# Issuing the first gate and value weights behind the third pair's cast instead of the fourth's

## The chip, the cores and the metric

The kernel runs on one core of a Trainium2 chip. The metric is the device time of one execution in microseconds; the time of a kernel is the median of its runs. Five engines work side by side, each through its own queue in order: TensorE (PE, with its weight loads PEld), VectorE (DVE), ScalarE (ACT), GpSimd (POOL) and SyncE (SP, which here only issues DMAs). POOL issues DMAs too: those that cast float32 to float16 on the way.

## The reference

Two attentions over the same q, k and v are added, and the sum goes through a gated feed-forward layer. Shapes: 8 batches, 8 heads, 576 positions, head size 64; the layer takes 4608 tokens of 512 through 1536 hidden columns.

```python
q_d = q.reshape(B, H, Sd, 4, D).mean(axis=3)      # k_d, v_d alike
out_up = np.repeat(sm_attn(q_d, k_d, v_d), 4, axis=2)
mask = np.abs(pos[:, None] - pos[None, :]) < 4
attn = softmax(np.where(mask, scale * q @ k.T, -1e9))
attn_out = out_up + attn @ v
x = attn_out.transpose(0, 2, 1, 3).reshape(B * S, H * D)
out = (np.maximum(x @ w_gate, 0.0) * (x @ w_val)) @ w_out
```

## The kernel before

The attention goes over 32 pairs of heads, four to a batch, numbered 0 to 31. For each pair: q and k are loaded (SP), cast to float16 and put in order (L1330 or L1329, tile `c`, for the first four pairs staged in `gT` and `wo_sb`), transposed (L1456 on PE for the first eight pairs, by DMA after that), copied out (`qkT`), summed over four positions (`qkd`), and multiplied to scores, local (L1518) and downsampled (L1537). The local scores become `s_sb` (minus the maximum), `e` (exponential) and are divided by their sum at L1610; the downsampled ones become `nmb` (L1590, the bias of the exponential), `wd` and are divided at L1626. `e` is turned by DVE (L1616, tile `at`), `wd` by PE (L1635) into `wT`. The value windows are 96 KB loads of small rows (L1675, tile `vw`, four a pair), cast at L1330 or L1329. The last product of a pair is L1726 with L1734; its result is added into `xT` (L1754).

The feed-forward layer takes tokens in stretches. A step is one of 128 hidden columns: four matmuls with gate weights and four with value weights (L1793, tiles `wg_sb` and `wv_sb`), the rectifier on ACT (L1807, tile `r`), the product on DVE (L1814, tile `gT`). Then 128 tokens at a time are multiplied with the output weights (L1859, `wo_sb`) and copied out (L1868). The stretch of batch 0 needs pairs 0 to 3, the next one pairs 4 to 7, and so on. The first two steps begin with the three pairs that are there (the columns of pairs 0 to 2) and add pair 3's columns later. The casts of pairs 4 to 7 wait for the divisions and for `wT` of pair 3.

The weights come by POOL in pieces: four of the gate (384 columns each), four of the value, four of the output. `W_AT` gives each pair of gate and value pieces the planned time before which it may not be issued.

The order on every engine is made when the kernel is built: `list_schedule` takes each operation with a duration, its dependencies, a rank (`prio`) and perhaps an earliest time (`after`). It steps through planned time and takes, on the engine that can start soonest, the lowest rank among what is ready. `RANKS` is a table of shifts by name added to the ranks (pair 3's cast has -489). Where an operation can run on several engines, the planner chooses the one that would end it first. The same order is then written out on each engine's queue.

Names used below: pair p's cast, its divisions (L1610 for `e`, L1626 for `wd`), its windows' cast (`vw`), its last product. "The second stretch" begins with the first gate step after batch 0's tokens.

Of the kernel before, what the change touches and what calls it, by code (L numbers as in the profile page):

```python
# [48 lines left out]

DMA_START = {SP: 0.8, POOL: 2.2}  # L50
RECEIPT = 1.2
W_AT = (20.0, 30.0, 34.0, 38.0)
WO_T0, WO_DT = 52.0, 6.0

PACE = (-10, -6, -5, 0)
# [1166 lines left out]
def kernel(  # L1222
# [90 lines left out]
    def add(*a, **kw):  # L1313
        o = Op(*a, **kw)
        ops.append(o)
        return o
# [62 lines left out]
    def wpiece(dst, src, c0, n):  # L1379
        return lambda o: nc.gpsimd.dma_start(  # L1380
            out=dst[:, :, c0 : c0 + n],
            in_=_dap(src, c0, [[DFF, 128], [128 * DFF, 4], [1, n]]))
# [6 lines left out]
    for g in range(4):  # L1389
        for nm, dst, src in (("g", wg_sb, moe_w_gate), ("v", wv_sb, moe_w_val)):  # L1390
            w_ld[nm, g] = add(POOL, 0.85, wpiece(dst, src, 384 * g, 384), prio=-40 + g,
                              xfer=2.55, after=W_AT[g], name=f"w{nm}{g}", port=(POOL,))

# [565 lines left out]
```

## Time and profile before

| what | us |
|---|---|
| median of three runs | 366.89 |
| lowest, highest run | 366.61, 369.45 |
| the profiled execution's own time | 368.73 |
| its span, first to last instruction | 367.0 |
| PE busy in the span | 352.3 |
| DVE, ACT, POOL busy | 254.4, 206.1, 199.6 |

The profile is one execution. Its span is 1.7 us shorter than its own time, and its own time is 1.8 us above the median; a change is worked out as a difference to 368.73 and then taken off the median. In the rows of the timeline the columns are start, duration, engine, line, operation, output<-input, shapes, count, and in brackets the idle time before it with what ended it. TensorE's granted clock was 1.00 throughout.

### The profile page before, as it was taken

The numbers are of one execution on the slowest core, as the hardware profiler recorded it, in microseconds if no ns is written. First come the engines' busy times: TensorE is split into PE (matmuls) and PEld (weight loads), VectorE is DVE, ScalarE is ACT, GpSimd is POOL, SyncE is SP. The second block draws the span as 40 slices with busy tenths as digits, with TensorE's granted clock in tenths as the row PEclk, the third lists the DMA queues.
The fourth block names the chain that finished last, engine by engine and source line by source line (L and its number), as shares of the span: only waits on it lengthen the run. The fifth ranks groups of instructions, "written<-read, shape, count | busy, mean of one in ns | idle before, by whom it ended". The sixth has DMA issues, their size and how long they took to land.

```text
span 367.0 us, 10494 instructions
## 1 busy us (share of the span) xinstructions
PE 352.3 (96%) x4238; PEld 181.9 (50%) x4238; DVE 254.4 (69%) x482; ACT 206.1 (56%) x481; POOL 199.6 (54%) x235
## 2 busy tenths in 40 slices
PE   7787999889999999999999999999989999999996
PEld 3444645445554554545444445544544454445554
DVE  4675999946889698878885986788968863322210
ACT  2576686436875657665466575768558533323222
POOL 7689566731567979675877469476885310000000
DMA  7999999669999999999999999999995121011012
GB/s 185 216 266 228 195 171 325 102 131 193 287 188 206 194 319 171 251 210 274 192 171 223 239 282 166 224 270 181 215 222 112 24 79 59 0 60 52 5 66 108
DMA packets 122067, 64.80 MB, mean 177 GB/s; under 512 B 100386, under 2 KB 106402, under 8 KB 122018
## 3 DMA queue, kind: packets, MB, share of 16 engines
q1 hardware_dynamic: 116194, 59.41, 74.8%
q0 software_dynamic: 5824, 4.72, 8.3%
q8 instruction: 33, 0.54, 0.7%
q14 instruction: 16, 0.13, 0.1%
HBM read 47.59 MB, written 9.44 MB: 155 GB/s over the span
## 4 chain that ended last, share of the span: by engine, by line
PE 78%; DMA 11%; DVE 4%; POOL 2%; issue 1%; ACT 1%; SPq 1%; POOLq 0%; ACTq 0%
PE bank L1793 49%; PE bank L1859 19%; DMA wg_sb<-in_moe_w_gate_dram 3%; DMA vw<-in_v_dram 3%; PE bank L1518 3%; PE bank L1726 2%; DMA tq<-c 2%; PE bank L1734 2%; DMA wT<-wd 2%; DMA sums_sb<-sums 1%; PE bank L1537 1%; DVE e L1610 1%; DVE vw L1352 1%; PE bank L1838 1%; DVE wd L1626 1%
## 5 line engine op out<-in xcount | busy, mean ns | idle before, releaser
L1814 DVE TENSOR_TENSOR gT<-r,bank 128x512 f16<-128x512 f16 (+1 forms) x112 | 74.5, 667 | 65.2 <-PE bank L1793 61.6
L1793 PE MATMUL bank<-xT,wg_sb 128*128 128x512 f16 (+2 forms) x528 | 112.1, 341 | 1.3 <-DMA wg_sb<-in_moe_w_gate_dram 1.3
L1793 PE MATMUL bank<-xT,wv_sb 128*128 128x512 f16 (+2 forms) x528 | 112.1, 341 | 0.8 <-ACT r L1807 0.8
L1807 ACT ACTIVATE r<-bank 128x512 f16<-128x512 f32 (+1 forms) x112 | 65.2, 583 | 64.1 <-PE bank L1793 57.8
L1859 PE MATMUL bank<-wo_sb,gT 128*128 128x512 f16 x420 | 96.7, 379 | 0.0
L1793 PEld LDWEIGHTS <-wg_sb 128*128 128x128 f16 x528 | 43.8, 98 | 48.0 <-DMA wg_sb<-in_moe_w_gate_dram 1.8
L1793 PEld LDWEIGHTS <-wv_sb 128*128 128x128 f16 x528 | 44.2, 98 | 46.2 <-issue 2.0
L1859 PEld LDWEIGHTS <-gT 128*128 128x128 f16 x420 | 39.9, 98 | 45.3 <-issue 0.4
L1868 ACT COPY y_sb<-bank 128x512 f32<-128x512 f32 x35 | 20.5, 586 | 47.9 <-PE bank L1859 45.6
L1330 POOL CAST vw<-vw 128x1536 f16<-128x1536 f32 x26 | 38.1, 1466 | 4.5 <-issue 1.4
L1506 DVE TENSOR_REDUCE qkd<-qkT 128x288 f16<-128x1152 f16 x28 | 37.5, 1339 | 4.1 <-ACT qkT L1329 3.9
L1600 ACT ACTIVATE wd<-bank,nmb 128x144 f16<-128x144 f32 x96 | 35.7, 381 | 4.9 <-POOL nmb L1590 3.2
L1616 DVE STREAM_TRANSPOSE at<-e 64x384 f16<-64x384 f16 x64 | 36.3, 568 | 2.7 <-POOL e L1610 1.8
L1581 POOL TENSOR_TENSOR s_sb<-s_sb,mx 128x384 f32<-128x384 f32 x28 | 23.3, 833 | 25.2 <-DVE mx L1578 23.3
L1610 POOL TENSOR_TENSOR e<-e,rs 128x384 f16<-128x384 f16 x31 | 25.9, 841 | 17.9 <-DVE rs L1608 16.2
L1626 POOL TENSOR_TENSOR wd<-wd,rsd 128x432 f16<-128x432 f16 x31 | 28.2, 912 | 11.2 <-DVE rsd L1622 11.2
L1754 DVE TENSOR_TENSOR xT<-bank,od_sb 128x288 f16<-128x288 f32 (+2 forms) x68 | 26.7, 431 | 7.4 <-ACT od_sb L1745 7.3
L1329 ACT COPY qkT<-tq 128x1152 f16<-128x1152 f16 x23 | 27.7, 1205 | 2.4 <-DMA tq<-c 2.4
L1712 POOL TENSOR_TENSOR vs<-v 104x512 f32<-104x512 f32 x20 | 25.4, 1271 | 4.9 <-DMA v<-in_v_dram 4.6
L1330 POOL CAST c<-qk 128x1152 f16<-128x1152 f32 x17 | 19.4, 1150 | 4.9 <-DMA tq<-c 2.0
L1717 POOL TENSOR_TENSOR vdz<-vs 104x256 f16<-104x256 f32 x20 | 14.6, 729 | 11.4 <-PE bank L1734 11.0
L1587 DVE TENSOR_REDUCE nmx<-bank 128x3 f32<-128x432 f32 x32 | 19.0, 593 | 2.5 <-PE bank L1537 2.2
(69 smaller groups left out, 349.6 us busy)
## 6 DMA issues: line engine op xcount, KB each, us to landing
vw<-in_v_dram SPq DMA_DIRECT2D x126, 96.0 KB, 4.6
out_dram<-y_sb SPq DMA_DIRECT2D x16, 512.0 KB, 4.2
qk<-in_q_dram SPq DMA_DIRECT2D x14, 576.0 KB, 6.1
qk<-in_k_dram SPq DMA_DIRECT2D x14, 576.0 KB, 6.5
v<-in_v_dram SPq DMA_DIRECT2D x10, 640.0 KB, 7.3
wv_sb<-in_moe_w_val_dram POOLq DMA_DIRECT2D x4, 384.0 KB, 11.3
wg_sb<-in_moe_w_gate_dram POOLq DMA_DIRECT2D x4, 384.0 KB, 11.2
wo_sb<-in_moe_w_out_dram POOLq DMA_DIRECT2D x4, 384.0 KB, 5.8
```

Source lines behind the costliest of these rows:

```text
L1329: return lambda o: nc.scalar.copy(out=dst, in_=src(o))
L1330: return lambda o: engine[eng].tensor_copy(out=dst, in_=src(o))
L1506: nc.vector.tensor_reduce(out=qkd[S3].rearrange("p (x t) -> p x t", x=2), in_=qk_sums, axis=AX.X, op=ALU.add)
L1600: exd.append(add(ACT, 0.37, lambda o, i=i: nc.scalar.activation(out=_sap(wd_, 0, 128, 256 * i + K0, kd_cols), in_=_sap(dview()[:, i, :], 0 ...
L1610: r["nrm"] = nrm = add_any(either(lambda o, e: e.tensor_tensor(out=e_, in0=e_, in1=bc12(rs[S3]), op=ALU.mult), (POOL, 0.84), (DVE, 0.5)), ...
L1616: tr.append(add(DVE, 0.575, lambda o, lo=lo: nc.vector.transpose(out=at2[S3][lo : lo + 64, :, lo // 2 : lo // 2 + 32], in_=e_[lo : lo + 64 ...
L1626: r["nrd"] = nrd = add_any(either(lambda o, e: e.tensor_tensor(out=_sap(wd_, 0, 128, K0, w3), in0=_sap(wd_, 0, 128, K0, w3), in1=_sap(rsd[ ...
L1754: nc.vector.tensor_tensor(out=xT[:, kk, (c1 + lo) % XR : (c1 + lo) % XR + hi - lo].rearrange("p (t f) -> p t f", f=4), in0=bank[V.banks[hf ...
L1793: nc.tensor.matmul(out=bank[(h or o).banks[0]][:, n * x : n * x + n], lhsT=w_sb[:, kk, bass.ts(jj, 128)], rhs=xT[:, kk, x_col(t0) : x_col( ...
L1807: rl = add(ACT, 0.17 + 0.00083 * n * m, lambda o: nc.scalar.activation(out=rt[:, 0 : n * m], in_=bank[f1.banks[0]][:, 0 : n * m], func=AF. ...
L1814: gm = add(DVE, 0.15 + 0.00104 * n * m, lambda o: nc.vector.tensor_tensor(out=gT[:, js[0] : js[0] + m, pos : pos + n], in0=rt[:, 0 : n * m ...
L1859: nc.tensor.matmul(out=bank[parts[0].banks[0]], lhsT=gT[:, jj, col : col + 128], rhs=wo_sb[:, jj, :], start=(jj == 0), stop=(jj == NJJ - 1))
```

## The change

One number of the planner's table of earliest times: the first gate piece and the first value piece may be issued from planned time 14 on, not 20. The ranks, the durations and all operations stay.

```diff
-W_AT = (20.0, 30.0, 34.0, 38.0)
+W_AT = (14.0, 30.0, 34.0, 38.0)
```

The number is used here; `after` is a floor of the planned start:

```python
for g in range(4):
    for nm, dst, src in (("g", wg_sb, moe_w_gate), ("v", wv_sb, moe_w_val)):
        w_ld[nm, g] = add(POOL, 0.85, wpiece(dst, src, 384 * g, 384), prio=-40 + g,
                          xfer=2.55, after=W_AT[g], name=f"w{nm}{g}", port=(POOL,))
```

With rank -40 the two pieces now come up before the ranks of the first pairs' small operations, and what the planner does after them changes on POOL, DVE, ACT and PE until the second stretch begins; SP's order stays the same in the whole program.

On POOL before, from the casts of pairs 0 to 2 (first row; pair 3's is the last `wo_sb` row) to the first two pieces. `nmb` are the biases of pairs 0 and 1, `vw_84` and `vw_85` the window casts of the same pairs, `e_92` and `e_93` their divisions, and the ISA row goes with the first bias (L1590):

```order
L1330 CAST wo_sb<-gT 96x2x12x64 x3
L1590 ISA
L1590 TENSOR_SCALAR nmb_129<-nmx_126 128x3
L1330 CAST vw_85<-vw_65 128x1536
L1590 TENSOR_SCALAR nmb_130<-nmx_127 128x3
L1330 CAST vw_84<-vw_64 128x1536
L1610 TENSOR_TENSOR e_92<-e_92,rs_123 128x384
L1610 TENSOR_TENSOR e_93<-e_93,rs_124 128x384
L1330 CAST wo_sb<-gT 96x2x12x64
L1380 DMA wv_sb<-in_moe_w_val_dram 128x4x384
L1380 DMA wg_sb<-in_moe_w_gate_dram 128x4x384
```

And now:

```order
L1330 CAST wo_sb<-gT 96x2x12x64 x3
L1380 DMA wv_sb<-in_moe_w_val_dram 128x4x384
L1380 DMA wg_sb<-in_moe_w_gate_dram 128x4x384
L1590 ISA
L1590 TENSOR_SCALAR nmb_129<-nmx_126 128x3
L1590 TENSOR_SCALAR nmb_130<-nmx_127 128x3
L1610 TENSOR_TENSOR e_92<-e_92,rs_123 128x384
L1610 TENSOR_TENSOR e_93<-e_93,rs_124 128x384
L1330 CAST vw_84<-vw_64 128x1536
L1330 CAST vw_85<-vw_65 128x1536
L1330 CAST wo_sb<-gT 96x2x12x64
L1590 TENSOR_SCALAR nmb_131<-nmx_128 128x3
```

The two DMA issues moved from behind pair 3's cast to the front of pair 0's bias; the two divisions moved from behind the window casts to the front of them; pair 3's cast stands behind all of these.

On DVE before, at the end of batch 0's steps (`r_78` is a late step's product there); `wd_101` at the top is pair 5's division, `e_92` further down pair 6's, the `at` rows turn the pairs' `e`:

```order
L1626 TENSOR_TENSOR wd_101<-wd_101,rsd_137 128x6x3x24
...
L1814 TENSOR_TENSOR gT<-r_78,bank_140 128x512
L1616 STREAM_TRANSPOSE at_88<-e_93 64x12x32 x2
L1606 TENSOR_REDUCE sm_120<-e_92 128x12
L1608 RECIPROCAL rs_123<-sm_120 128x12
L1610 TENSOR_TENSOR e_92<-e_92,rs_123 128x384
L1616 STREAM_TRANSPOSE at_87<-e_92 64x12x32 x2
L1754 TENSOR_TENSOR xT<-bank_142,od_sb_113 128x288
L1754 TENSOR_TENSOR xT<-bank_144,od_sb_113 128x288
```

And now, from pair 6's sum to the added products of pair 7:

```order
L1616 STREAM_TRANSPOSE at_87<-e_92 64x12x32 x2
L1814 TENSOR_TENSOR gT<-r_78,bank_140 128x512
L1606 TENSOR_REDUCE sm_121<-e_93 128x12
L1608 RECIPROCAL rs_124<-sm_121 128x12
L1754 TENSOR_TENSOR xT<-bank_142,od_sb_112 128x288
L1754 TENSOR_TENSOR xT<-bank_143,od_sb_112 128x288
L1616 STREAM_TRANSPOSE at_88<-e_93 64x12x32 x2
L1754 TENSOR_TENSOR xT<-bank_145,od_sb_113 128x288
L1754 TENSOR_TENSOR xT<-bank_142,od_sb_113 128x288
```

Neither division stands on DVE any more (in the whole order DVE has none now; both went to POOL, while the window cast of pair 4 went from POOL to ACT and that of pair 7 from ACT to POOL), and pairs 6 and 7 come in turn, where pair 7 came first.

On ACT before, around the first rectifiers (`r_77`, `r_78`); `c` are the casts of pairs 4 and 5 and, now, of pair 7:

```order
L1329 CAST c_83<-qk_61 128x2x9x64
L1329 CAST c_82<-qk_61 128x2x9x64
L1745 ACTIVATE od_sb_113<-bank_145 128x144
L1329 COPY qkT_116<-bank_143 128x128x4
L1329 COPY qkT_115<-bank_143 128x128x5
L1807 ACTIVATE r_77<-bank_141 128x512
L1807 ACTIVATE r_78<-bank_139 128x512
```

And now:

```order
L1329 CAST c_83<-qk_61 128x2x9x64
L1329 CAST c_82<-qk_61 128x2x9x64
L1329 CAST vdz_96<-bank_144 96x2x2x64
L1329 COPY qkT_116<-bank_145 128x128x4
L1745 ACTIVATE od_sb_113<-bank_142 128x144
L1329 COPY qkT_115<-bank_143 128x128x5
L1329 COPY qkT_115<-bank_145 128x128x4
L1329 CAST c_82<-qk_62 128x2x9x64
L1807 ACTIVATE r_77<-bank_138 128x512
L1807 ACTIVATE r_78<-bank_139 128x512
```

Pair 7's cast moved from POOL to ACT, in front of the first rectifier, and one more copy of pair 4 to `qkT` stands in front of it too.

From the second stretch on the five orders are the same as before, but for pair 11's scores, which stand one product earlier on PE, and their masking on DVE.

## The prediction

> **What bounds the kernel now.** I read the page first, then the table of windows, then who waits for whom on PE, then the timelines of the engines that PE waits for. The page:
>
> ```profile
> PE 352.3 (96%) x4238; PEld 181.9 (50%) x4238; DVE 254.4 (69%) x482; ACT 206.1 (56%) x481; POOL 199.6 (54%) x235
> ```
>
> PE is busy but for 14.7 us. The windows show where the idle time lies (second column pair: PE; last two: DMA share and GB/s):
>
> ```profile
> 30.00:40.00 10.00, 8.09 (x142) 4.78 (x140) 5.60 (x13) 5.91 (x10) 8.52 (x10) 1.00 1.28 205
> 40.00:50.00 10.00, 10.00 (x171) 5.93 (x162) 9.50 (x16) 7.42 (x18) 5.27 (x6) 1.00 1.28 194
> 50.00:60.00 10.00, 10.00 (x219) 5.73 (x218) 8.63 (x17) 6.89 (x22) 6.65 (x8) 1.00 0.99 255
> 60.00:70.00 10.00, 8.50 (x75) 4.39 (x74) 9.30 (x17) 6.58 (x17) 6.10 (x8) 1.00 0.89 189
> 70.00:80.00 10.00, 8.66 (x76) 4.56 (x75) 7.22 (x11) 2.59 (x7) 6.74 (x6) 1.00 0.68 129
> 80.00:100.00 20.00, 20.00 (x277) 9.97 (x276) 13.58 (x22) 14.73 (x31) 6.38 (x8) 1.00 0.96 212
> 260.00:280.00 20.00, 18.75 (x297) 9.62 (x294) 15.67 (x31) 13.01 (x31) 15.12 (x18) 1.00 1.10 199
> ```
>
> After the start PE idles 1.50 us in 60 to 70 and 1.34 us in 70 to 80; 80 to 100 is full, and the only loss that I find between that and the end is 1.25 us in 260 to 280. So the kernel is: a start of some 35 us in which PE waits for data, two stalls while pairs 4 to 7 are finished, then matmuls almost without a gap. The end moves by what the beginning of the second stretch moves. The waits of PE name the stalls:
>
> ```profile
> PE bank L1635 <- DVE wd L1626: 1.5, 1, 1.5
> PE bank L1726 <- DVE at L1616: 1.3, 1, 1.3
> PE bank L1793 <- DMA wg_sb<-in_moe_w_gate_dram: 1.3, 1, 1.3
> ```
>
> The third is for the weights that the change moves, the first two are in the region that it re-plans. In the timelines of DVE and POOL (start, duration) both come from a DVE division that takes many times its length:
>
> ```profile
> 62.98 2.53 DVE L1626 TENSOR_TENSOR wd<-wd,rsd 128x432 f16<-128x432 f16 x1
> 71.49 3.05 DVE L1610 TENSOR_TENSOR e<-e,rs 128x384 f16<-128x384 f16 x1
> 63.56 1.48 POOL L1330 CAST vw<-vw 128x1536 f16<-128x1536 f32 x1
> 72.65 1.47 POOL L1330 CAST vw<-vw 128x1536 f16<-128x1536 f32 x1
> 67.22 0.83 POOL L1610 TENSOR_TENSOR e<-e,rs 128x384 f16<-128x384 f16 x1 [2.18 <-DVE rs L1608]
> 68.81 0.90 POOL L1626 TENSOR_TENSOR wd<-wd,rsd 128x432 f16<-128x432 f16 x1
> ```
>
> The two divisions end 0.4 to 0.5 us after a POOL cast beside them ends (65.51 against 65.04, 74.54 against 74.12); on POOL the same work takes 0.83 and 0.90 us. DVE's divisions were held up by POOL's casts.
>
> **The change part by part. First the start.** POOL's queue there, with DVE's reciprocal of pair 0's sum among it:
>
> ```profile
> 12.80 1.47 POOL L1330 CAST wo_sb<-gT 96x1536 f16<-96x1536 f32 x1 [2.37 <-DMA gT<-in_q_dram]
> 16.20 0.23 DVE L1608 RECIPROCAL rs<-sm 128x12 f32<-128x12 f32 x1
> 17.21 1.46 POOL L1330 CAST vw<-vw 128x1536 f16<-128x1536 f32 x1 [1.03 <-DVE rs L1608]
> 18.64 1.62 POOL L1610 TENSOR_TENSOR e<-e,rs 128x384 f16<-128x384 f16 x2
> 20.21 1.46 POOL L1330 CAST wo_sb<-gT 96x1536 f16<-96x1536 f32 x1
> 21.61 0.98 POOL L1380 DMA_DIRECT2D wv_sb<-in_moe_w_val_dram  x1
> 22.59 0.76 POOL L1380 DMA_DIRECT2D wg_sb<-in_moe_w_gate_dram  x1
> 30.15 1.48 POOL L1330 CAST vw<-vw 128x1536 f16<-128x1536 f32 x1
> 31.59 0.91 POOL L1626 TENSOR_TENSOR wd<-wd,rsd 128x432 f16<-128x432 f16 x1
> ```
>
> The third pair's cast ends at 14.27. Now the two issues come there, 0.98 + 0.76 = 1.74 us, so pair 0's bias waits until 16.0 and its three exponentials on ACT with it; the divisions of pairs 0 and 1 follow at 16.4 (the reciprocal is there by 16.43) to 18.0, two us sooner than the 18.64 of before; then the two window casts, 2 x 1.46, and pair 3's cast can start at 20.9 instead of 20.21. But it also needs its k, and the weights now run beside that load:
>
> ```profile
> L1430 SPq DMA_DIRECT2D gT<-in_k_dram x1: 1333/1333/1333, 14.0 to 14.0; - x1
> DMA to landing us min/median/max: 5.6/5.6/5.6
> 17.58 0.47 SPq L1675 DMA_DIRECT2D vw<-in_v_dram  x1
> 36.42 3.84 SPq L1675 DMA_DIRECT2D vw<-in_v_dram  x2
> ```
>
> It landed at 14.04 + 5.6 = 19.6 with no weights in flight. A window load was issued every 0.47 us then; in 36 to 40, with weights in flight, every 1.92 us, four times slower. Between the start of the weights (about 15.3) and the end of that load stand one window load, which at that price costs 1.45 us more, and large rows of q and k, for which I assume 0.9 us more (nothing in the rows gives it). I take 22.0, an estimate with 20.9 as the lower end (nothing is delayed beyond POOL's own queue) and 25.1 as the upper: each weight piece takes 2.7 us of the line (the issue of 22.59 landed 12.4 us later, at 35.0, that of 29.31 after 8.4 us, at 37.7), and two whole pieces in front of the load are 5.4 us.
>
> ```profile
> L1380 POOL DMA_DIRECT2D wg_sb<-in_moe_w_gate_dram x1: 825/825/825, 29.3 to 29.3; - x1
> DMA to landing us min/median/max: 8.4/8.4/8.4
> 22.59 12.38 DMA wg_sb<-in_moe_w_gate_dram
> ```
>
> The Trainium skill (DMA: Bandwidth & Descriptors, "Queues, rings and completion order") says that each DMA engine goes round between the queues that have work, a packet at a time; by that rule small rows pay most, which is what the four times slower windows show, and the load of large rows would be nearer to my estimate than to the upper end.
>
> From pair 3's cast to its division of `wd` (20.21 to 31.59) POOL's queue loses the two issues (1.74) and pair 3's window cast (1.48, now behind the division) and gains pair 2's window cast (1.46, was on ACT): 1.76 us less. With the cast 1.8 us later the division falls where it was, and of the 1.2 us that POOL idled in that stretch some 0.8 us go, since its inputs are there sooner: the division and `wT` of pair 3 come 0.8 us sooner, and so do the casts of pairs 4 and 5 that wait for them. The first gate weights are there by 15.3 + 12.4 = 27.7 at the price of before, so the wait of 1.3 us on them goes, but it is replaced by pair 3's chain; I count nothing for it.
>
> Then ACT: the third `qk` cast now stands in front of the first rectifier.
>
> ```profile
> 33.66 2.20 ACT L1329 CAST c<-qk 128x1152 f16<-128x1152 f32 x2
> 39.15 1.09 ACT L1807 ACTIVATE r<-bank 128x512 f16<-128x512 f32 x2
> ```
>
> A cast is 1.1 us. The third step on PE needs the bank that the first rectifier empties; with the rectifier 1.1 us behind its place and PE with two transposes and one score to spare, I get a wait of 0.85 us there. So 0.8 - 0.85: the start gives nothing.
>
> **Then the two stalls.** Neither division is on DVE now. On POOL pair 5's costs 0.90 and pair 6's 0.83 us, and POOL in 40 to 80 is busy 24.8 of 40 us, so there is room for these, for pair 7's window cast (+1.47) less pair 7's `qk` cast (-1.15) and pair 4's window cast (-1.48). DVE, busy 34.7 of 40, loses 5.6 us. Following the new order with the durations above, pair 6's `at` is done about 1 us before PE comes to its last product and pair 7's 1.7 us before; these are what is late next. Both stalls go: 1.50 + 1.34 = 2.84 us.
>
> The Trainium skill (SBUF — State Buffer, "Who interferes with whom") has it that a DVE operation with two SBUF inputs is fully blocked by a GpSimd operation that reads SBUF, and the other way round; the trace agrees with its 2.53 and 3.05 us. By that rule no further such block is left in this region, since DVE's remaining products there read a bank.
>
> **Then the second stretch.** Its order is the same as before. It keeps the gain if no other engine is fixed in time there:
>
> ```profile
> 80.65 1.03 PE L1793 MATMUL bank<-xT,wg_sb 128*128 128x512 f16 x4
> 82.65 0.69 DVE L1814 TENSOR_TENSOR gT<-r,bank 128x512 f16<-128x512 f16 x1 [4.97 <-PE bank L1793]
> 90.01 0.83 POOL L1581 TENSOR_TENSOR s_sb<-s_sb,mx 128x384 f32<-128x384 f32 x1 [10.38 <-DVE mx L1578]
> SPq L1487 <- POOL c L1330: 13.4, 2, 12.5
> ```
>
> At its beginning DVE waits 4.97 us for PE and POOL 10.38 us for DVE, and SP waited 12.5 us for pair 8's cast, which comes earlier with pair 7. DMA has room too (0.68 in 70 to 80). So all moves together.
>
> Sum: -0.8 + 0.85 - 2.84 = -2.8 us: 368.73 - 2.8 = 365.9 in the profiled execution's own time, 366.89 - 2.8 = 364.1 against the median.
>
> **The rivals.** (1) More is won: k lands before POOL gets to pair 3's cast. Then the start is 1.1 us sooner, and if the 0.85 us behind ACT's cast is hidden too: 364.1 - 1.95 = 362.1. For it: DMA was half idle in 20 to 22, so the loads that follow have room.
>
> ```profile
> 20.00:22.00 2.00, 1.63 (x21) 0.69 (x18) 1.91 (x5) 1.41 (x2) 2.00 (x3) 1.00 0.55 118
> ```
>
> Its share was 0.55 there. Against it: the windows' price. Chance 0.17.
>
> (2) No change: the work that POOL takes over makes pair 6 or 7 late, and PE waits 2.8 us there as before, or the later pairs give it back. For it: POOL gets five operations in a row for pairs 6 and 7. Against it: a margin of 1 to 1.7 us. 366.9. Chance 0.17.
>
> (3) Slower: the load of pair 3's k is behind both weight pieces and lands at 25.1. In POOL's queue that cast stands before the divisions of pairs 0 to 2, so all wait 3.1 us more than in my forecast; the casts of pairs 4 to 7 wait for pair 3, so the stalls at pairs 6 and 7 stay too: 366.89 + 3.1 = 370.0. It decides from a landing of 22 on if the stalls stay, from 25 on if they go. Chance 0.2.
>
> That the change does not do what it says is excluded by the order on POOL.
>
> **How the numbers follow.** The forecast has 0.46, and its own range is 362.9 to 365.4. A difference of less than 1% (3.7 us) is about what a measurement of this kernel can't tell from no change. Faster by more, under 363.2: rival 1 whole and 0.13 of the forecast, 0.30. Slower by more, over 370.6: 0.12 of rival 3. The rest, 0.58, is within. The range from 361.8 to 369.9 leaves out a third of rival 1 below and half of rival 3 above, some 0.17.
>
> **What would show it.** Right: no `wd` or `e` division on DVE with 2.5 us or more; no wait of PE on L1635 or L1726; the second stretch's first gate step at about 77.8; the end moved by as much. Wrong in the start: pair 3's cast on POOL waiting on the k load past 22, and the casts of pairs 4 and 5 after 33.66. Wrong in the second part: PE waiting at L1726 on `at` or `vdz` between 60 and 76. Wrong in the last: the stretch starts sooner but waits of PE on DMA or ACT appear after 80.

## The result, and the profile after

| what | before | now |
|---|---|---|
| median of the comparison | 366.92 (11 runs) | 365.50 (11 runs) |
| lowest, highest | 366.41, 369.45 | 363.79, 366.96 |
| ratio, 95% interval | | 0.995 (0.9927 to 0.9974) |
| the profiled execution's own time, its span | 368.73, 367.0 | 365.24, 363.5 |
| first gate step of the second stretch | 80.65 | 77.48 |

The kernel is faster by 1.4 us in this comparison (1.0 to 2.7 by the interval), and by 2.4 us in a second one (ratio 0.994, 0.9916 to 0.9964, below). Forecast were 2.8.

The page of the changed kernel:

```profile
PE 352.8 (97%) x4241; PEld 182.2 (50%) x4241; DVE 248.4 (68%) x477; ACT 206.9 (57%) x484; POOL 201.4 (55%) x237
```

The table of windows, first of before, then of the changed kernel (start:end, length, then busy time and count of PE, PEld, DVE, ACT, POOL; the clock; DMA share; GB/s):

```profile
0.00:36.00 36.00, 28.49 (x505) 16.04 (x506) 22.35 (x52) 19.95 (x51) 28.82 (x40) 1.00 1.01 224
36.00:60.00 24.00, 24.00 (x473) 14.29 (x470) 21.17 (x36) 16.81 (x43) 14.45 (x17) 1.00 1.16 221
60.00:80.00 20.00, 17.17 (x149) 8.96 (x148) 16.52 (x27) 9.17 (x23) 12.84 (x13) 1.00 0.78 159
```

```profile
0.00:36.00 36.00, 30.61 (x510) 17.23 (x511) 22.05 (x50) 20.11 (x54) 29.83 (x41) 1.00 1.09 226
36.00:60.00 24.00, 23.33 (x471) 14.31 (x469) 22.01 (x40) 19.48 (x48) 13.72 (x17) 1.00 1.21 221
60.00:80.00 20.00, 19.59 (x184) 9.69 (x169) 10.25 (x22) 8.39 (x20) 14.30 (x15) 1.00 0.83 174
80.00:180.00 100.00, 100.00 (x1377) 51.01 (x1375) 83.84 (x157) 64.14 (x152) 68.60 (x79) 1.00 1.08 225
250.00:285.00 35.00, 33.85 (x437) 16.90 (x436) 29.29 (x56) 22.66 (x54) 24.61 (x29) 1.00 0.93 167
```

Up to 60 us PE idles 7.51 us before and 5.39 + 0.67 = 6.06 now: 1.45 less. From 60 to 80 it idles 2.83 before and 0.41 now: 2.42 less. Not all of the first is won, since some of PE's busy time is matmuls of zeros (L1360) that only keep it going. The groups by line, before and now:

```profile
L1360 PE MATMUL bank<-r 128*128 128x512 f16 x50 | 14.2, 413 | 1.6 <-DVE mx L1352 1.2 <-DVE s_sb L1571 0.2 <-issue 0.2
```

```profile
L1360 PE MATMUL bank<-r 128*128 128x512 f16 x53 | 14.8, 419 | 1.7 <-DVE mx L1352 1.2 <-issue 0.5
```

That is 0.6 us more of them. So the start won 1.45 - 0.6 = 0.8 us and the two stalls 2.4, together 3.2, and by as much the second stretch begins sooner (80.65 - 77.48 = 3.17):

```profile
77.48 1.03 PE L1793 MATMUL bank<-xT,wg_sb 128*128 128x512 f16 x4
```

The 0.41 us that PE idles in 60 to 80 stand at 60:

```profile
60.69 0.19 PE L1518 MATMUL bank<-qkT 64*32 64x32 f16 x2 [0.41 <-issue]
```

The waits of PE of the changed kernel name no division on DVE any more, and none on the gate weights; what is left on a division is 0.6 us for POOL's (0.7 before):

```profile
PE bank L1456 <- POOL wo_sb L1330: 1.1, 3, 0.5
PE bank L1690 <- POOL vw L1330: 0.9, 2, 0.7
PE bank L1793 <- ACT r L1807: 0.9, 1, 0.9
PE bank L1518 <- DVE xT L1754: 0.7, 1, 0.7
PE bank L1635 <- POOL wd L1626: 0.6, 2, 0.4
```

POOL's timeline at the start:

```profile
14.15 0.97 POOL L1380 DMA_DIRECT2D wv_sb<-in_moe_w_val_dram  x1
15.12 0.76 POOL L1380 DMA_DIRECT2D wg_sb<-in_moe_w_gate_dram  x1
16.60 1.62 POOL L1610 TENSOR_TENSOR e<-e,rs 128x384 f16<-128x384 f16 x2 [0.15 <-DVE rs L1608]
18.17 2.88 POOL L1330 CAST vw<-vw 128x1536 f16<-128x1536 f32 x2
20.99 1.46 POOL L1330 CAST wo_sb<-gT 96x1536 f16<-96x1536 f32 x1
26.01 1.46 POOL L1330 CAST vw<-vw 128x1536 f16<-128x1536 f32 x1
30.50 0.91 POOL L1626 TENSOR_TENSOR wd<-wd,rsd 128x432 f16<-128x432 f16 x1
```

Pair 3's cast starts at 20.99 right behind the window casts, with no bracket: its k was there. Pair 3's division is at 30.50, 1.09 us sooner than the 31.59 of before. The load of that k on SP, and the five window loads behind it with their time to landing:

```profile
13.97 1.57 SPq L1430 DMA_DIRECT2D gT<-in_k_dram  x1
```

```profile
L1675 SPq DMA_DIRECT2D vw<-in_v_dram x5: 542/589/1372, 15.6 to 18.5; - x5
...
DMA to landing us min/median/max: 7.7/8.2/8.3
```

ACT's third cast, and the rectifier behind it:

```profile
33.12 2.21 ACT L1329 CAST c<-qk 128x1152 f16<-128x1152 f32 x2
...
38.39 1.16 ACT L1329 CAST c<-qk 128x1152 f16<-128x1152 f32 x1
39.43 1.11 ACT L1807 ACTIVATE r<-bank 128x512 f16<-128x512 f32 x2
```

### The profile page after: what moved, and what is told of

The parts are those of the page before. It is cut to its first block, busy times and chain, and to the rows that moved or that the text cites. A ratio compares the mean times of both kernels' runs of the same rounds, so it can differ in the third digit from the quotient of the medians.

```text
span 363.5 us, 10504 instructions
## 1 busy us (share of the span) xinstructions
PE 352.8 (97%) x4241; PEld 182.2 (50%) x4241; DVE 248.4 (68%) x477; ACT 206.9 (57%) x484; POOL 201.4 (55%) x237
## 4 chain that ended last, share of the span: by engine, by line
PE 85%; DMA 4%; POOL 3%; SPq 2%; issue 2%; DVE 1%; ACT 1%; POOLq 0%; ACTq 0%; DVEq 0%
PE bank L1793 50%; PE bank L1859 23%; PE bank L1518 4%; DMA vw<-in_v_dram 3%; PE bank L1726 2%; PE bank L1734 2%; PE bank L1537 2%; DMA gT<-in_q_dram 1%; POOL vw L1330 1%; SPq L1675 1%; PE bank L1635 1%; PE bank L1690 1%; POOL wd L1626 1%; PE bank L1838 1%; PE bank L1456 1%
## 5 line engine op out<-in xcount | busy, mean ns | idle before, releaser
L1330 POOL CAST vw<-vw 128x1536 f16<-128x1536 f32 x27 | 39.5, 1463 | 3.6 <-DMA vw<-in_v_dram 2.3
L1610 POOL TENSOR_TENSOR e<-e,rs 128x384 f16<-128x384 f16 x32 | 26.8, 841 | 16.6 <-DVE rs L1608 12.6
L1626 POOL TENSOR_TENSOR wd<-wd,rsd 128x432 f16<-128x432 f16 x32 | 29.1, 910 | 9.9 <-DVE rsd L1622 9.7
L1330 POOL CAST c<-qk 128x1152 f16<-128x1152 f32 x16 | 18.2, 1149 | 5.2 <-issue 2.8
```

The source lines that it names most:

```text
L1330: return lambda o: engine[eng].tensor_copy(out=dst, in_=src(o))
L1610: r["nrm"] = nrm = add_any(either(lambda o, e: e.tensor_tensor(out=e_, in0=e_, in1=bc12(rs[S3]), op=ALU.mult), (POOL, 0.84), (DVE, 0.5)), ...
L1626: r["nrd"] = nrd = add_any(either(lambda o, e: e.tensor_tensor(out=_sap(wd_, 0, 128, K0, w3), in0=_sap(wd_, 0, 128, K0, w3), in1=_sap(rsd[ ...
```

## The experiments

In the expectations, P is the theory that the stalls of before were a matter of its one profiled execution, and Q that they are the same in every one. S is the theory that the changed kernel's start varies from execution to execution, and T that the second stretch begins at the same time in all of them and that the rest of a difference comes from waits after it. What is compared is above all the start of the second stretch's first gate step, where the orders come together again; in three executions of each kernel it was at 80.65, 81.36 and 80.97 before and at 77.48, 78.04 and 77.78 now.

| kernel | first gate step | median (runs) | before beside it | ratio, interval |
|---|---|---|---|---|
| b1_before_again | 81.36 | 367.82 (1) | 367.12 | |
| b2_before_again | 80.97 | 368.63 (1) | 367.12 | |
| a1_after_again | 78.04 | 365.43 (6) | 367.86 | 0.994, 0.9916 to 0.9964 |
| a2_after_again | 77.78 | 366.71 (1) | 367.86 | |
| div_on_pool | 78.78 | 366.12 (12) | 367.12 | 0.9969, 0.994 to 0.9997 |
| weights_alone | 82.41 | 369.23 (10) | 367.12 | 1.0059, 1.004 to 1.0078 |
| weights_alone_busy | 82.50 | 372.04 (6) | 367.56 | 1.0123, 1.0084 to 1.0161 |
| issue_no_traffic | 81.50 | 368.24 (12) | 366.99 | 1.0016, 0.9983 to 1.0049 |
| after_late_weights | 82.29 | 367.94 (12) | 367.86 | 1.0007, 0.998 to 1.0034 |
| late_weights_busy | 80.50 | 369.41 (12) | 367.56 | 1.0055, 1.0025 to 1.0086 |
| after_div_on_dve | 76.72 | 365.61 (12) | 366.99 | 0.9961, 0.994 to 0.9981 |
| after_wg1_later | 77.66 | 365.65 (12) | 366.99 | 0.9952, 0.9929 to 0.9976 |

### Both kernels again

No edit.

> The kernel before, unchanged, profiled a second time. Theory P: the profiled execution that the prediction read (368.73 us) was not a typical one; its two long DVE divisions (2.53 and 3.05 us) and the waits of PE behind them (1.50 and 1.34 us) depend on which of DVE and POOL comes first and are shorter in an execution near the median. Then this profile, at a time near 366.9, has its second stretch beginning at about 79 instead of 80.65 and PE waits of about 1.0 us together at L1635 and L1726. Rival Q: the stalls are the same in every execution, and the time differs somewhere after 80; then the second stretch begins at 80.5 or later also here.

> The same as the run before it, a third profile of the kernel before. P: the beginning of the second stretch and the execution's time move together, from profile to profile, by up to 2 us, and the DVE divisions in 60 to 75 are what differs. Q: the beginning of the second stretch is the same within 0.3 us whatever the time.

> The changed kernel, unchanged, profiled and timed again beside the kernel before. Theory S (the start varies): in an execution near the median of 365.5 the second stretch begins later than at 77.5, between 78.5 and 79.5, because the loads of the first 30 us land differently; the gain at that point is then 1.5 to 2 us. Rival T (the tail varies): the second stretch begins at 77.5 within 0.3 us in every profile, and what an execution loses against 363.8 lies in waits of PE between 185 and 205 and between 260 and 280, where the first profiles of both kernels show 0.2 to 1.2 us. The ratio comes out between 0.993 and 0.998 again.

> A third profile of the changed kernel. S: its second stretch begins at another time than the others', by 0.5 us or more, and pair 3's scores differ as much. T: it begins at 77.5 within 0.3 us and the profiles differ only after 185.

Both stalls are there in all three executions of before (1.5 and 1.3 us), so P falls. The first gate step varies more than Q and T allowed (they had 0.3 us): by 0.71 us in before and by 0.56 in the changed kernel. Its mean is 80.99 before and 77.77 now: 3.2 us apart, with no overlap. Behind it the executions differ. Busy PE in 180 to 210, 210 to 250 and 250 to 285, of before's second repetition and of the changed kernel's:

```profile
180.00:210.00 30.00, 29.29 (x388) 14.31 (x386) 22.70 (x42) 17.55 (x40) 22.32 (x25) 1.00 1.04 198
210.00:250.00 40.00, 40.00 (x523) 19.97 (x522) 32.25 (x63) 26.76 (x64) 25.46 (x30) 1.00 1.07 235
250.00:285.00 35.00, 35.00 (x400) 17.66 (x399) 30.73 (x61) 24.91 (x57) 26.65 (x31) 1.00 0.99 192
```

```profile
180.00:210.00 30.00, 28.67 (x385) 14.02 (x384) 22.85 (x42) 17.45 (x40) 20.40 (x24) 1.00 1.04 201
210.00:250.00 40.00, 39.21 (x475) 19.77 (x474) 31.43 (x65) 26.77 (x63) 26.18 (x31) 1.00 1.13 232
250.00:285.00 35.00, 35.00 (x443) 17.53 (x442) 30.64 (x59) 24.94 (x57) 25.72 (x31) 1.00 0.95 186
```

From 80 to 285 us PE lost 1.31, 0.00 and 0.71 us in the three executions of before, and 1.15, 0.56 and 2.12 in those of the changed kernel: a mean of 0.7 and of 1.3. Most of it in the worst of them are two waits for the transposed `wd`:

```profile
185.64 0.41 PE L1734 MATMUL bank<-wT,vdz 104*128 104x144 f16 x4 [1.06 <-DMA wT<-wd]
229.97 0.41 PE L1734 MATMUL bank<-wT,vdz 104*128 104x144 f16 x4 [0.79 <-DMA wT<-wd]
```

So 3.2 us are won at 80, some 0.6 is given back on the average of three, and the spans differ by 366.6 - 364.0 = 2.6. T holds but for its 0.3 us; S, which had the second stretch at 78.5 to 79.5 in a1_after_again, does not. Whether the changed kernel loses more there as a rule, or three executions are too few, stays open, and so does what makes these transfers late.

### The two divisions moved alone

In before's order, pair 5's division of `wd` and pair 6's of `e` run on POOL; nothing else moves.

```diff
+    for o in order:
+        if o.name in ("nrd5", "nrm6"):
+            o.eng, o.dur, o.emit = next(x for x in o.alts if x[0] == POOL)
     owners = [o for o in order if o.banks]
```

> The order of before, with nothing moved but the two DVE divisions of pairs 5 and 6, which run on POOL at the same place of the order. Theory P: the two stalls are worth about 1.0 us in a median execution, so 366.9 - 1.0 = 365.9, and no DVE division is in its trace. If the stalls are worth what the prediction took (2.84 us), 364.1. If POOL, which now has to do both between its casts, hands the wait on to pairs 6 and 7 (rival 2 of the prediction), 366.9 or more.

Both stalls go, and two smaller waits come: 0.48 us at 64.22 for pair 5's division on POOL (in the first row, of which 0.7 us stood before too), and one for output weights, whose issue now stands later on POOL (at 71.03, before at 69.66; waits of PE):

```profile
PE bank L1635 <- POOL wd L1626: 1.2, 3, 0.6
PE bank L1859 <- DMA wo_sb<-in_moe_w_out_dram: 0.8, 1, 0.8
```

The first gate step is at 78.78, 1.9 us sooner than in before's profile; the median gains 1.0 with an interval of 0.1 to 2.2. Moving the divisions away does take the stalls, and this part of the change can be had without any other.

### The weights moved alone

In before's order the first two pieces are issued behind the third cast.

```diff
+    third = next(i for i, o in enumerate(order) if o.name == "cast2")
+    early = [o for o in order if o.name in ("wv0", "wg0")]
+    order = [o for o in order if o not in early]
+    order[third + 1:third + 1] = early
     owners = [o for o in order if o.banks]
```

> The order of before, with nothing moved but the first two weight issues, which come behind the third pair's cast as in the changed kernel; no other operation changes its place. The prediction's first step gives: pair 0's bias 1.74 us later, the wait of PE on the gate weights (1.3 us) gone, and nothing in the time, 366.5 to 367.2. If the weights' DMAs hold up the k load of pair 3 (rival 3), its cast on POOL waits past 22 and the time is 368 or more. If PE's wait on the weights was on the path by itself, 365.6.

It is slower by 2.1 us. The early issue that the diff asks for is, taken by itself, a loss. ACT's cast of a window waits for its load, and PE for that cast (timelines of ACT and PE):

```profile
25.16 1.47 ACT L1329 CAST vw<-vw 128x1536 f16<-128x1536 f32 x1 [2.71 <-DMA vw<-in_v_dram]
26.68 0.40 PE L1690 MATMUL bank<-vw,sums_sb 128*32 128x256 f16 x6 [2.35 <-ACT vw L1329]
```

The five window loads issued from 15 to 19 us, first in before, then here (the last line is the time from issue to landing):

```profile
L1675 SPq DMA_DIRECT2D vw<-in_v_dram x5: 413/467/589, 15.4 to 17.6; - x5
...
DMA to landing us min/median/max: 4.0/4.6/4.6
```

```profile
L1675 SPq DMA_DIRECT2D vw<-in_v_dram x5: 512/774/1622, 13.7 to 18.1; - x5
...
DMA to landing us min/median/max: 7.9/8.1/8.3
```

The weights' traffic makes them land some 3.5 us later. Pair 3's k, which the expectation feared for, landed after 5.9 us (5.6 in before). In the changed kernel the windows are as slow (median 8.2), but there pair 2's window is cast by POOL at 26.01, behind five other operations, and nobody waits. The granted clock fell in this execution, though, twice, each time behind a long wait of PE:

```profile
16.00:18.00 2.00, 0.28 (x5) 0.15 (x2) 0.55 (x3) 1.38 (x7) 1.89 (x4) 0.85 0.92 132
18.00:20.00 2.00, 2.00 (x5) 0.44 (x3) 1.55 (x6) 2.00 (x9) 2.00 (x3) 0.50 1.25 268
28.00:30.00 2.00, 2.00 (x34) 1.60 (x22) 1.75 (x5) 1.70 (x7) 0.40 (x1) 0.50 1.05 301
```

That is another reading of the same loss, C, against D, the queue and the windows. The next kernel tells them apart: 9 matmuls of zeros before the two steps that wait (5 and 1 stood there), into a bank that is free.

```diff
-                if o.fill and spare:
+                if o.name in ("VP0", "VP2"):
+                    emit_zeros(spare[-1], 9)
+                elif o.fill and spare:
                     emit_zeros(spare[0], o.fill)
```

> weights_alone's profile has a granted clock of 0.85, 0.50 and 0.79 in 16 to 22 us and of 0.91, 0.50 and 0.73 in 26 to 32, each behind a stretch of two us in which PE was busy for 0.28 and 0.33; before's and the changed kernel's start has 1.00 throughout. Here PE is kept busy in these two gaps by 9 matmuls of zeros each, into a bank that nobody waits for. Theory C (the clock is what weights_alone loses): 1.00 throughout the start, the second stretch 1.5 us or more ahead of weights_alone's 82.41, the median at about 367.5 instead of 369.2. Theory D (POOL's 1.74 us and the slower windows are on the path, and the slow clock falls on steps for which nobody waits, since PE waited 2.35 us for a window cast between the two drops): 1.00 as well, but the second stretch within 0.4 us of 82.4 and the median within 0.7 of 369.2.

The clock is 1.00 from 14 to 46, and the first gate step is at 82.50 against 82.41, where C needed 80.9 or less. The slow clock had cost nothing that is seen there; PE waited for the window in any case (1.18 us for ACT's cast). D holds at that point. The median doesn't answer: it is 372.04, not lower but higher. The profiled execution is the longest of its six (376.22), and in it a new wait stands further on, in an order that differs by the added instructions alone; behind this wait the clock is at 0.50 from 142 to 148 (timeline of PE):

```profile
142.52 1.87 PE L1793 MATMUL bank<-xT,wv_sb 128*128 128x512 f16 x4 [3.38 <-issue]
```

### The issues without the traffic

In before's order two more issues stand behind the third cast. Each loads 8 of a piece's 384 columns, a second time and with the same values; the whole pieces stay where they were.

```diff
+    third = next(i for i, o in enumerate(order) if o.name == "cast2")
+    for dst, src in ((wg_sb, moe_w_gate), (wv_sb, moe_w_val)):
+        small = Op(POOL, 0.85, wpiece(dst, src, 0, 8), name="small")
+        small.start, small.end = order[third].start, order[third].end
+        order.insert(third + 1, small)
     owners = [o for o in order if o.banks]
```

> The order of before with every operation where it was, and two additional weight issues of 8 columns each behind the third pair's cast: POOL's time of the earlier issue without its traffic (the full pieces stay where they were and write the same values again). The kernel with the weights alone moved was 2.1 us slower. If that came from the traffic, which made pair 2's window loads land 8 us after their issue and not 4.5, so that ACT waited 2.7 us for them, this kernel is at 367 to 367.5 beside 367.1, and ACT does not wait for windows. If it came from the 1.74 us that pair 0's bias is later, it is 1.5 to 2 us slower than the kernel before.

The windows land after 4.9 to 5.6 us, and ACT's window cast waits 0.22 us and not 2.71: it is the traffic that makes them late. The first gate step is at 81.50, 0.85 behind before's; the clock was at 0.50 from 20 to 24 here too. That would make 0.85 the most that POOL's lost time costs, and 0.9 of weights_alone's 1.76 (82.41 - 80.65) the traffic. These are single executions, though, and those of one kernel lie up to 0.7 us apart at this point, so the split is an estimate. In the median (ratio 1.0016, with 1 inside its interval) nothing can be told.

### The new order with the weights late

In the changed kernel's order the two issues stand behind pair 3's cast again.

```diff
+    early = [o for o in order if o.name in ("wv0", "wg0")]
+    order = [o for o in order if o not in early]
+    fourth = next(i for i, o in enumerate(order) if o.name == "cast3")
+    order[fourth + 1:fourth + 1] = early
     owners = [o for o in order if o.banks]
```

> The order of the changed kernel, with nothing moved but the first two weight issues, which stand behind pair 3's cast again, as before. If the earlier issue itself is worth something in the new order, PE waits at its first gate step for the weights (issue at about 21, landing 10 to 12 us later, 32 to 33.5, against a first step at 32.6): 0 to 1 us, so 365.5 to 366.5. If the whole gain is the new order's and the early issue costs what it cost in the old one (about 2 us there), this kernel is the fastest: 363.5 to 364.5, with pair 3's cast at 19.3 and the divisions of pairs 0 and 1 from 14.9 on.

Expected were 365.5 to 366.5, or the fastest kernel of all, and the gain is gone: 367.94 against 367.86 of before. The two stalls are gone here as well (PE idles 0.52 us from 46 to 84), so the start loses all that they give. Pairs 2 and 3 now stand behind the 1.7 us of issues (pair 2's bias at 24.62, in the changed kernel at 22.43), and the weights are late (PE):

```profile
25.81 0.54 PE L1635 MATMUL bank<-ident_sb,wd 128*96 128x128 f16 x6 [1.63 <-POOL wd L1626]
35.86 1.46 PE L1793 MATMUL bank<-xT,wg_sb 128*128 128x512 f16 x3 [1.45 <-DMA wg_sb<-in_moe_w_gate_dram]
```

The three matmuls of the second row take 1.46 us, in the changed kernel 0.81. The windows show why:

```profile
34.00:36.00 2.00, 0.55 (x6) 0.21 (x4) 1.09 (x3) 1.77 (x3) 2.00 (x3) 0.88 1.31 248
36.00:38.00 2.00, 2.00 (x6) 0.59 (x4) 0.00 (x0) 0.97 (x1) 2.00 (x4) 0.50 1.30 216
38.00:40.00 2.00, 2.00 (x20) 0.87 (x19) 0.48 (x1) 0.62 (x2) 1.88 (x2) 0.77 1.29 216
```

The clock was halved for 3.4 us (0.24 + 1.00 + 0.46 are missing, at half speed twice as long). So this one was filled too, with 7 matmuls of zeros (1 stood there) before the first gate step:

```diff
-                if o.fill and spare:
+                if o.name == "hg0_0a":
+                    emit_zeros(spare[-1], 7)
+                elif o.fill and spare:
                     emit_zeros(spare[0], o.fill)
```

> after_late_weights' profile has a granted clock of 0.88, 0.50 and 0.77 in 34 to 40 us, behind the wait of 1.45 us on the gate weights; the first gate steps take 1.46 us there instead of 0.81. Here PE is kept busy before the first gate step by 7 matmuls of zeros into a bank that nobody waits for. Theory C: 1.00 in 34 to 40, and the second stretch 1.5 us ahead of after_late_weights' 82.29 (half of the 3.3 us at half clock, on steps that stand in a row), the median at 367.0 to 367.5 instead of 367.9, since only 5 of its 12 runs had a mean clock of 0.995 or less. Theory D (the issues between pair 3's cast and pairs 2 and 3's small operations, and the wait on the weights): the clock back, the second stretch within 0.5 us of 82.3, the median within 0.3 of 367.9.

Here the two theories share it. The clock is at 1.00 in 34 to 40, and the first gate step comes 1.8 us sooner, at 80.50: these steps are on the path, and in the profiled execution of after_late_weights (370.51, the longest of its 12) the clock had cost about that. It is still 2.7 us later than in the changed kernel (77.77): that is the queue with what stands behind it, and whatever a fall of the clock at another place (24 to 28) adds here, which was not told apart. The median is not lower (369.41), and PE waits where it had not. The clock is not what keeps after_late_weights from a gain: seven of its twelve executions had a mean clock of 0.999 or more, and their median is 367.51. The new wait:

```profile
139.06 0.38 PE L1793 MATMUL bank<-xT,wv_sb 128*128 128x512 f16 x1 [1.26 <-issue]
```

### The new order with the divisions on DVE again

```diff
+    for o in order:
+        if o.name in ("nrd5", "nrm6"):
+            o.eng, o.dur, o.emit = next(x for x in o.alts if x[0] == DVE)
     owners = [o for o in order if o.banks]
```

> The order of the changed kernel, with nothing moved but the divisions of pairs 5 (wd) and 6 (e), which run on DVE at the same place of the order. By the prediction's second term they are held up by POOL's operations there as before, and both stalls come back: 2.5 to 3 us slower than the changed kernel, that is 368.0 to 368.5. If the new order leaves PE enough other work at those places (pairs 4 and 5 are done four to eight us sooner), the divisions are long but PE does not wait: 365.5.

Expected in the first place were the stalls, and they do not come back. DVE's two divisions and POOL's beside the second:

```profile
52.51 0.61 DVE L1626 TENSOR_TENSOR wd<-wd,rsd 128x432 f16<-128x432 f16 x1
64.93 0.55 DVE L1610 TENSOR_TENSOR e<-e,rs 128x384 f16<-128x384 f16 x1
64.97 1.28 POOL L1626 TENSOR_TENSOR wd<-wd,rsd 128x432 f16<-128x432 f16 x1
```

They take 0.61 and 0.55 us, not 2.53 and 3.05: neither runs beside a cast of POOL in this order. The second one comes just before a division of POOL, and now that one is held up, 1.28 us instead of 0.91. The first gate step is at 76.72, sooner than in any other kernel, and the median is the changed kernel's (365.61). That is the time of the second expectation, but not its reason: the divisions are not long.

### The second gate piece later

On the changed kernel, its issue (28.82) moved behind pair 3's division.

```diff
+    one = next(o for o in order if o.name == "wg1")
+    order.remove(one)
+    order.insert(next(i for i, o in enumerate(order) if o.name == "nrd3") + 1, one)
     owners = [o for o in order if o.banks]
```

> The order of the changed kernel, with nothing moved but the second gate piece, which is issued on POOL behind pair 3's two divisions and not in front of them. The runs so far say that POOL's time between pair 3's cast and its division of wd is on the path to the first gate steps and to the casts of pairs 4 and 5. Then 0.85 us less there gives 0.4 to 0.8 us: 364.7 to 365.1 beside 365.5. If PE's first steps are bound by pair 2's products (the adds at 32.4) or the weights, nothing: 365.5. If the second piece then lands behind its use (the fourth gate step at 41.8), 366 or more.

Pair 4's scores come 0.7 us sooner, and it is given back before the second stretch: 77.66, 365.65, the nothing of the expectation. No kernel of the study is clearly faster than the changed one.

## Why the prediction was right, and where it was off

**The second stretch moves as a whole: right.** Forecast 77.8, measured 77.48, 78.04 and 77.78. PE is full from 80 to 180, and L1734 of every pair from 8 to 18 stands 3.17 to 3.19 us sooner than in before's profile.

**The two stalls: right in what goes, off in the reason and in the size.** 2.84 were to go; 2.42 went, since 0.41 of a new wait stands at 60. The reason given was that the divisions leave DVE. div_on_pool shows that this would do; after_div_on_dve shows that it wasn't needed, since the new order no longer starts a division on DVE while POOL casts. What held DVE up was POOL's work at the same time, as the prediction read from 62.98 and 71.49, and either way out of it works. It was more than the one cast beside each, though: the second division lasted through two casts (`c` from 71.56, `vw` from 72.65), and the first began while POOL issued output weights (62.72 to 63.56). Whether that issue holds DVE up by itself was not tried.

**The start: the term was mis-sized, 0 instead of 0.8.** The prediction had pair 3's cast at 22.0, for which k's load was to land 2.4 us later; the 0.9 of it for the large rows stands in no row. It started at 20.99 and waited for nothing: k needed at most 7.0 us (issued at 13.97; 5.6 before), not 8. The small rows of the windows paid for the weights beside them (a median of 4.6 us before, 8.2 now), the large rows of k with 1.4 us at most, and with 0.3 in weights_alone, where POOL waited for that load and its landing stands in the trace (5.9). So rival 1's condition was met, but little of its 1.1 us came: pair 3's division was to be at 30.8 by the forecast and at 29.7 by rival 1, and it is at 30.50 (before 31.59). ACT's third cast (38.39) pushed the first rectifier from 39.15 to 39.43 only, not by its own 1.1 us, since the two casts ahead of it came 0.54 sooner (33.66 to 33.12) and ACT idled 0.72 us on the way and not 1.63. The third step on PE waits for nothing: it is at 40.10, before at 40.15, and by then PE has done nine more transposes (L1456 of tile `c`, 27 and not 18). So the 0.85 counted for a wait there was too much, and the start's gain is work that is done sooner.

**The sum: 3.2 at the second stretch against 2.8 forecast; 1.4 to 2.4 in the medians.** The start's 0.8 and the 0.4 that the stalls gave less make 0.4 more at 80 than forecast; that 77.8 came as near as it did is in part luck, since the two errors pull against each other. After it the prediction let everything move alike. The three executions of each kernel lost 0.7 and 1.3 us there, which brings 3.2 down to 2.6; that much is measured. The rest, to 1.4 and 2.4, is within what the intervals leave (1.0 to 2.7 and 1.3 to 3.1). The 365.50 lies just above the forecast's own range (362.9 to 365.4), midway between 364.1 and no change; the wide range holds no change as well, so the median alone does not bear the forecast out, and the start of the second stretch does. One thing the prediction could have seen: it subtracted from a median what was read in an execution 1.8 us above that median. And the 1% that it took for the least that can be told was too coarse: these intervals reach 0.9 us to either side.

**The rivals.** No change, and slower by a late k, are both out, though rival 2's later pairs do give some 0.6 us back. What rival 3 feared exists: weights_alone is slower by 2.1 us. The traffic does delay what runs beside it, the windows far more than k. In the new order pair 2's window cast stands late on POOL (26.01) and nobody waits for it; that this place is what saves it is read from the traces and was not tried alone. The new order without the early issue gains nothing either (after_late_weights): its stalls are gone, and its start loses as much. The two moved divisions alone gain 1.0 us (0.1 to 2.2); the rest of the gain is of the early issue and the order together.

## What to carry to other kernels

An issue on a compute engine's queue costs its own time there (0.76 to 0.97 us a piece here) and slows the small-row loads beside it; ask who stands behind it in the queue and who waits for those loads, before asking when its data is needed. A change of one planner's number is a new order: price the order, and try the number and the order apart, since here the early issue alone lost 2.1 us and the order without it gained nothing. To compare such kernels read the point where the orders come together again, in several executions; the end of the program adds waits that come and go (0 to 2.1 us of PE's time here) and are nearly as large as the effect.

## What the runs showed of the hardware that I had not expected

**The clock falls behind short waits, sometimes.** PE idle for 1.45 us (34.41 to 35.86) in after_late_weights was followed by 3.4 us at half clock; an idle stretch of 1.63 us at 24.2 in the same execution was not, and one of 1.62 at the same place in the program was, in late_weights_busy. The Trainium skill (TensorE: Matmul & The Clock Gate, "Part 1: The HAM clock gate") has the clock halved after an idle window of about 3.4 us, and full again after a busy one of that length, in a window that runs free of the program. The time at half clock and the chance in it agree with these rows, but waits of half that length were enough here; whether the thin work around them counts too (PE was busy for 0.55 us in 34 to 36) was not tried.

**Two kernels with more matmuls of zeros have a wait 100 us later.** With 12 and 6 more of them before 36 us, PE waits 3.38 and 1.26 us at about 140 for nothing that the profile shows, where before and the changed kernel are full. In the kernels that they were made from, weights_alone and after_late_weights, PE is full there too, so the added instructions are all that is new. In both a load of instructions (queue q8) stands some 3 us before PE goes on (in 139.5 to 140.0 and in 136.0 to 136.5); the kernels without the wait have such loads too (in 137.0 to 138.0), so that PE waited for its instructions is a guess. Each was profiled once, and what the wait is was not tried.

**DVE and POOL hold each other up in both directions.** Beside POOL's casts DVE's divisions take 2.53 and 3.05 us, without them 0.55 to 0.61; and a division of POOL that starts 0.04 us behind one of DVE takes 1.28 instead of 0.91.
